# Second product last in the last pair, its last store on ScalarE's queue, two warm-up matmuls fewer, and all steps in another order

## The chip, the core and the metric

The kernel runs on one core of a Trainium2 chip. The core has a matrix engine (TensorE, in the profile PE, its weight loads PEld), a vector engine (VectorE, DVE), an activation engine (ScalarE, ACT), a general engine (GpSimd, POOL) and a queue engine that issues most transfers (SyncE, SP). Each takes its own instructions in program order and waits on semaphores for the others. The metric is the device time of one execution in microseconds. The kernel before took 226.16 us, the median of 3 runs (226.01 to 226.32).

## The reference

One transformer layer on 2048 tokens of width 640, in bf16: layer norm, linear attention with 32 heads of width 20 and a softmax feature map, a residual, a second layer norm, and a feed-forward part of width 1728 with SiLU.

```
h  = x + A(layernorm(x))          # A: q, k, v = x @ wqkv
                                  #    phi(u) = [softmax(u @ w_phi), softmax(-(u @ w_phi))]
                                  #    kv = sum_s phi(k) v ; z = sum_s phi(k)
                                  #    o = phi(q) kv / (phi(q) z + 1e-6) ; o @ wo
h2 = h + silu(layernorm(h) @ w1) @ w2
```

## The kernel before

The 2048 tokens are 16 tiles of 128. The program is built of some nine hundred small named steps, each a function that emits a few instructions. A list, `ORDER` (lines 18 to 61), written out by hand or by a search outside the kernel, gives the order in which the steps are emitted, and so the order of the instructions on each engine; nothing else reorders them. Several functions take PSUM banks from a ring in the order in which they are called (lines 124 to 147), so `ORDER` also decides which step waits for which bank.

The steps that the text names:

- `warm0` and on (line 229): matmuls on a constant, 128x256, whose result nobody reads. There are `WARM = 20` (line 150), 18 at the very beginning, one after `fk2` and one before `fk0`.
- `X0, X1, X2, X4, X8`, `WK0` to `WK4`, `WV0` to `WV4`, `wq0` to `wq5`, `wph0`, `wph1`, `load0` to `load10`: loads, all issued from SP. `wq` are loads that transpose (line 425). `X8` brings the tokens 8 to 15 of every partition, 1280 KB.
- `wk0` to `wk4` (line 323): five TensorE transposes each of a part of the key weights `Wk`; `wke0` to `wke4` copy them out of PSUM. `fk0` to `fk4` (line 339) multiply them by the block-diagonal feature weights `phi`, `fk0e` to `fk4e` copy the result into `Wfk`. `fq0` to `fq5` with `fq0e` to `fq5e` do the same for the queries, from `phq` and `wq`.
- `st{t}` (line 474): mean and variance of tile t on VectorE. `rs{t}`: their inverse root, on GpSimd or ScalarE. `xn{t}`: the normalised tile. `xt{t}`: its transpose, by TensorE for the first four (copied out by `x{t}`), by a DMA from SP for the others.
- `K{t}`, `V{t}` (line 566): key and value projections, ten matmuls each. `ex{t}` (ScalarE) exponentials, `su{t}` (VectorE) their sums, `rk{t}` (ScalarE) the reciprocals, `sc{t}` (VectorE, line 641) the scaling, `ve{t}` (ScalarE) the values out of PSUM, `kv{t}` (line 656) the eleven matmuls that add tile t into the key-value sums. `kv{t}` needs `sc{t}`.
- `own`, `mask`, `mask0`, `mask1`, `ones0` to `ones6`, `pad0`, `ref5` to `ref15`: constants and buffer resets on GpSimd. `ref{t}` writes again into the buffer of keys that tile t-5 used, so it waits for `kv{t-5}`. `eqr0`, `eqr1` (line 457) write the constant slots of `EQ`, the buffer of the queries' exponentials.
- `Q{t}` (line 705): query projections; `qe{t}` exponentials, `qs`, `ql`, `qi`, `qr` sums and scaling, `qt{t}` the transpose by DMA. `D{t}`, `E{t}`, `ot{t}`: attention, division, transpose. `G{t}0`, `G{t}1`, `ga{t}`: output projection and residual. `lm, ls, lr, hn, ht`: the second layer norm and its transpose.
- `u{a}.{f}`, `s{a}.{f}`, `lt{a}` (lines 924 to 981): the first feed-forward product, SiLU, and the transpose of its last rows.
- The second feed-forward product works on pairs of tiles with Strassen's scheme in Winograd's form, seven products instead of eight: `T` (sums of weights), `S1` to `S4` (sums of tokens, on VectorE), `p1` to `p7` (products, seven matmuls each, line 1024), `r1, r2, r3, r7` (a product plus the residual, out of PSUM, line 1041), `w11, w12, w21, w22` (the four quarters of the output, line 1048). Products accumulate: `p1`, then `p6`, then `p5` go into one bank "a", and `r1`, `r2`, `r3` read it after the first, second and third; `p7` and `p4` share bank "d"; `p2` and `p3` have banks of their own, and only `w11` reads `p2`, only `w12` reads `p3`.
- `out{t}` (line 983): the store of a tile's output, from SP. In the last pair (t = 14) the store of tile 14 is cut into `out140`, `out141`, `out142`, and product p3 with its quarter w12 into two parts, `p3.14` (192 columns) and `p3.14x` (128 columns), `w12.14` and `w12.14x`.

Of the kernel before, what the change touches and what calls it, by code (L numbers as in the profile page):

```python
# [18 lines left out]
warm0 warm1 warm2 warm3 warm4 warm5 warm6 warm7 warm8 warm9 warm10 warm11 warm12 warm13 warm14 pad0
warm15 warm16 X0 WK2 st0 WK3 warm17 WK0 phi_a X1 wk2 own wke2 phi_b wk3 fk2 rs0 xn0 warm18 ones0 WK1  # L20
mask wke3 WK4 X2 WV0 wk0 wk1 fk2e WV3 wke0 st1 xt0 wke1 rs1 wk4 fk3 X4 fk3e x0 fk1 wke4 xn1 ones1 warm19
st2 fk0 wq4 WV2 V0.0 fk1e WV1 fk4 ones4 xt1 fk0e K0s st3 mask0 V0.3 fk4e x1 WV4 ones3 K0.2 K0.1 K0.0
wph0 K0.4 rs3 rs2 st4 K0.3 K1 V0.2 xn2 xt2 st5 ex0 rs4 ex1 V0.1 wph1 x2 V1 X8 ve1 xn3 xt3 su0 st6 rk0
xn4 V0.4 su1 x3 load10 ones5 wq0 sc0 K2 st7 rs5 st9 ve0 V2 xn5 rs6 xt4 xn6 ex2 rk1 sc1 ve2 ones2 rs9
st12 wq3 xt5 phq V3 kv0 rs7 ve3 xt6 K3 K4 xn7 V4 ref5 kv1 ex3 ex4 st8 rs8 su2 su3 ve4 fq0 fq0e V5 fq3
ref6 st10 rk2 xn8 ve5 wq2 K5 xn9 rk3 xt7 fq3e sc2 ex5 K6 ex6 kv2 wq1 sc3 su4 kv3 ref7 V6 su5 fq2 rk4 ve6
K7 V7 rs12 fq2e ref8 su6 xn12 sc4 kv4 fq1 rs10 ex7 ve7 xt8 st15 rk6 ones6 xt9 fq1e zeros V8 st11 su7 fq4
xn10 st14 ref9 ve8 rs11 wq5 sc6 rk5 fq4e xt12 xt10 rk7 V9 load7 sc5 ve9 K8 xn11 K9 sc7 fq5 kv5 fq5e kv6
load3 kv7 ex8 ex9 st13 rs14 rs13 eqr0 su8 Q0 qe0 su9 ref10 rk8 rk9 xn13 K10 ref12 xn14 ex10 xt11 V10 sc8
ve10 ref11 load9 Q1 kv8 V12 rs15 xn15 xt13 K12 qs0 qe1 su10 sc9 kv9 rk10 ve12 ref13 K11 load1 ex12 K13  # L30
ex11 sc10 qs1 su12 xt14 ql0 ex13 ql1 V11 su11 su13 eqr1 rk12 rk11 load4 qi0 ve11 kv10 K14 xt15 sc11 rk13
V13 ref14 sc12 eqp qr0 qi1 ex14 ve13 qr1 sc13 ref15 K15 load0 Q2 ex15 load2 kv11 kv12 su14 kv13 su15 V15
qe2 qt0 rk14 qt1 rk15 V14 sc14 ve14 sc15 mask1 load8 ve15 Q3 qs2 kv14 ql2 kv15 Q5 bd0 qe3 qe5 Q7 bd1
load5 qi2 halves qr2 qe7 D0 D1 qs3 ql3 E0 load6 Q4 qe4 Q10 qi3 qt2 E1 qr3 qs5 qe10 qs4 ql5 Q6 qe6 ot0 D2
ot1 Q9 qe9 qi5 ql4 qr5 E2 G00 G01 ga0 lm0 ls0 qi4 G11 G10 qt3 Q11 qs6 qr4 D3 ga1 qe11 qt5 E3 lm1 lr0 hn0
Q8 ls1 D5 ot2 qt4 Q13 qr6 G20 qs7 lr1 G21 qe8 hn1 Q14 qe13 E5 Q15 qe14 ot3 Q12 ga2 G31 G30 ht0 qe15 qe12
padL0 qs8 ht1 D4 u0.L ot5 T1.2 T1.0 qr7 s0.L T1.1 u0.0 lm2 padL1 qt6 ga3 E4 qt7 u0.6 qs9 G50 s0.0 qr8
lm3 G51 T2.1 s0.6 D6 u0.4 ls2 s0.4 ga5 E6 u0.8 D7 ot4 lr2 lm5 qt8 u0.10 T3.2 u0.2 E7 G41 G40 ls5 hn2
u0.12 ot6 s0.2 T2.2 D8 lr5 s0.8 T3.1 T3.0 lt0 ls3 S3.0 s0.10 ga4 hn5 E8 s0.12 ot7 T2.0 p7.0 S1.0 G61
p1.0 T4.1 S2.0 p2.0 r1.0 r7.0 G60 ht2 p6.0 T4.0 T4.2 lr3 p4.0 G71 S4.0 r2.0 p3.0 lm4 p5.0 qr9 ls4 lr4  # L40
G70 ga6 hn3 ht5 w21.0 qs11 hn4 w22.0 ga7 ht3 ht4 u2.L lm6 u2.9 s2.L u2.1 qt9 r3.0 u2.7 ot8 w11.0 lm7
w12.0 lt2 qr11 u2.10 s2.9 qs10 G81 qt11 s2.1 qr10 qs12 D9 u2.3 s2.3 s2.7 qt10 G80 E9 u2.5 ls6 lr6 u2.4
s2.10 u2.2 ga8 u2.6 D10 ls7 u2.0 ot9 qr12 qt12 qs13 u2.12 s2.4 E10 lm8 D11 hn6 s2.5 ls8 ot10 u2.8 s2.0
qs14 E11 s2.6 s2.12 lr7 lr8 u2.11 G90 qr13 s2.2 D12 hn7 hn8 S3.2 ht6 s2.8 G91 p7.2 G101 qr14 ga9 s2.11
S1.2 p1.2 S2.2 E12 G100 r1.2 out0 p2.2 ga10 qt13 ot11 lm9 p6.2 qt14 S4.2 D13 r2.2 r7.2 G110 G111 w11.2
ls9 out1 S3.4 p4.2 E13 p5.2 ot12 ga11 lr9 w21.2 ht7 hn9 ht9 ht8 w22.2 ot13 D14 p7.4 r3.2 E14 lm11 p3.2
qs15 S1.4 p1.4 S2.4 ls11 G121 r1.4 lm10 u6.L ls10 G120 u6.8 lr10 p6.4 r7.4 p4.4 ga12 S4.4 r2.4 lm12 qr15
G131 w12.2 ot14 w21.4 G130 ga13 qt15 s6.L hn10 ls12 ht10 p5.4 lr11 s6.8 u6.11 G140 lm13 hn11 s6.11 u6.4
s6.4 lr12 D15 G141 u6.2 hn12 ls13 out3 r3.4 w22.4 p2.4 u6.5 s6.5 s6.2 E15 ga14 lr13 hn13 u6.1 w11.4 ht12
u6.0 u6.3 lt6 u6.10 u6.7 out2 s6.10 s6.7 s6.3 s6.1 p3.4 w12.4 ht11 ht13 u6.6 s6.0 u10.L ot15 u6.12 u10.2  # L50
s6.12 u10.9 s10.L G151 G150 s6.6 u6.9 S3.6 s10.2 u10.11 s6.9 S1.6 ga15 S2.6 lm15 u10.0 p7.6 s10.9 p1.6
u10.6 lt10 lm14 S3.8 r1.6 s10.0 r7.6 s10.11 u10.7 s10.6 s10.7 u10.12 p4.6 S4.6 p6.6 p2.6 s10.12 r2.6
p5.6 r3.6 ls15 w11.6 w21.6 u10.5 p2.8 S1.8 ls14 u10.3 w22.6 out5 lr15 u10.1 s10.5 p7.8 lr14 p1.8 S2.8
s10.3 hn14 u10.4 hn15 s10.1 r1.8 s10.4 ht14 w11.8 S3.10 p3.6 p6.8 ht15 r7.8 S4.8 u10.8 p4.8 out4 u14.4
r2.8 w21.8 w12.6 s14.4 u10.10 p5.8 s10.8 w22.8 p3.8 r3.8 out6 u14.2 out9 w12.8 s14.2 s10.10 S1.10 u14.12
p7.10 u14.10 out7 u14.L s14.12 u14.0 u14.6 p1.10 out8 S3.12 s14.0 s14.L r7.10 lt14 u14.8 S2.10 r1.10
s14.6 p6.10 p4.10 s14.10 r2.10 p5.10 w21.10 r3.10 S4.10 p2.10 p7.12 p2.12 w11.10 w22.10 S1.12 p1.12
S2.12 r1.12 w11.12 p3.10 p6.12 r7.12 p4.12 S4.12 r2.12 S3.14 w21.12 s14.8 w12.10 p5.12 p1.14 out11 r3.12
# [6 lines left out]
def kernel(  # L65
# [160 lines left out]
    def add(name, emit):  # L226
        steps[name] = emit
# [752 lines left out]
            sh_l.pop(u)[:, 0:m].rearrange("p j f -> p (j f)"),  # L980
        )

    def store(t, a, b):
        nc.sync.dma_start(out_t[:, t, a:b], outs[t][:, a:b])

# [38 lines left out]
    def product(t, k, lo=0, hi=HD):  # L1024
        bank = INTO[k] + "x" * (lo > 0)
        if k in FIRST:
            ps_of[bank, t] = ps_half()
# [6 lines left out]
        right = {1: b11, 2: b21, 3: b22, 4: ws.get(4), 5: ws.get(1), 6: ws.get(2), 7: ws.get(3)}[k]
        for c in range(KS):
            nc.tensor.matmul(  # L1036
                ps[:, lo:hi], left[:, c, :], right[:, c, lo:hi], start=(c == 0 and k in FIRST),
                stop=(c == KS - 1 and k in LAST), skip_group_check=True,
            )
# [95 lines left out]
```

## Time and profile before

| | us |
|---|---|
| median of 3 runs | 226.16 (226.01 to 226.32) |
| the profiled execution | 226.19 |
| its span in the trace | 224.5 |
| TensorE busy | 219.7 (98%) |
| VectorE busy | 173.9 (77%) |
| ScalarE busy | 144.8 (65%) |
| GpSimd busy | 72.5 (32%) |
| chain that ended last, TensorE's share | 87% |
| the same, VectorE's share | 11% |

The span runs from the first instruction to the last; some 1.7 us of the execution lie outside it. A row of the timeline gives a start in microseconds from the start of the span, a duration, the engine, the line of the kernel, the operation, out<-in with the shape of one, and how many instructions of a line follow each other directly; a bracket at its end is the idle time of the engine before it and what ended that. DVEq, SPq and so on are the sequencer of an engine: waits, branches, and the issue of transfers. Matmuls overlap and their ends are modelled, so the time that one takes is read from the start of one to the start of the next.

### The profile page before, as it was taken

How to read it: one execution, taken by the hardware profiler on the slowest of the kernel's cores; microseconds unless marked ns; L12 is line 12 of the kernel's file. 1: busy time of each engine (PE TensorE's matmuls, PEld its weight loads, DVE VectorE, ACT ScalarE, POOL GpSimd, SP SyncE). 2: the span in 40 equal slices, each digit the busy share in tenths (PEclk: the TensorE clock that was granted, in tenths of full speed). 3: DMA queues.
4: the chain of work that ended last, by engine and by line, in shares of the span. 5: the costliest groups of instructions: out<-in, count | busy, mean ns of one | idle time of the engine just before them, and what ended most of it. 6: DMA issues, size and time to landing. Idle time of an engine off the chain costs nothing.

```text
span 224.5 us, 5053 instructions
## 1 busy us (share of the span) xinstructions
PE 219.7 (98%) x1937; PEld 155.1 (69%) x1937; DVE 173.9 (77%) x305; ACT 144.8 (65%) x321; POOL 72.5 (32%) x136
## 2 busy tenths in 40 slices
...
GB/s 171 293 357 81 92 95 86 204 243 145 286 222 191 164 144 90 163 90 114 121 119 131 112 174 128 44 123 101 72 53 0 0 4 88 92 29 10 29 50 99
DMA packets 68158, 26.98 MB, mean 120 GB/s; under 512 B 61159, under 2 KB 67111, under 8 KB 68007
## 3 DMA queue, kind: packets, MB, share of 16 engines
...
q10 hardware_dynamic: 656, 0.03, 0.2%
q14 instruction: 8, 0.07, 0.1%
...
## 4 chain that ended last, share of the span: by engine, by line
PE 87%; DVE 11%; issue 0%; DVEq 0%
PE banks L931 25%; PE banks L1036 23%; PE banks L571 11%; PE banks L849 10%; PE banks L609 9%; DVE st L478 4%; PE banks L817 3%; DVE Sk L630 2%; PE banks L662 2%; PE banks L231 2%; DVE xn L494 1%; DVE EK L643 1%; PE banks L942 1%; DVE mv L479 1%; DVE WTk L338 0%; PE banks L437 0%
## 5 line engine op out<-in xcount | busy, mean ns | idle before, releaser
L931 PE MATMUL banks<-HnT,w_sb 128*128 128x512 bf16 (+1 forms) x325 | 60.7, 336 | 0.0
L954 ACT ACTIVATE shT<-banks 128x512 bf16<-128x512 f32 (+1 forms) x53 | 29.5, 587 | 32.1 <-PE banks L931 31.9
L931 PEld LDWEIGHTS <-w_sb 128*128 128x128 bf16 x325 | 31.2, 98 | 21.2
L571 PEld LDWEIGHTS <-XnT 128*128 128x128 bf16 x300 | 28.7, 98 | 9.6
L494 POOL TENSOR_SCALAR xn<-X,mv,rs 128x640 bf16<-128x640 bf16 x12 | 32.4, 2701 | 1.6 <-ACT rs L485 1.3
L516 POOL TENSOR_SCALAR rs<-mv 128x1 f32<-128x1 f32 x16 | 3.5, 219 | 80.2 <-ACT xn L509 79.9
L1036 PEld LDWEIGHTS <-S 128*128 128x128 bf16 x231 | 22.1, 98 | 9.0
L1044 DVE TENSOR_TENSOR r<-banks,X 128x320 f32<-128x320 f32 x32 | 15.2, 486 | 15.9 <-PE banks L1036 15.5
L1036 PE MATMUL banks<-T,S 128*128 128x320 bf16 x168 | 26.7, 299 | 0.0
L849 PE MATMUL banks<-wo_sb,OT 128*128 128x320 bf16 x160 | 25.3, 299 | 0.0
L1051 DVE TENSOR_TENSOR o_t<-banks,r 128x320 bf16<-128x320 f32 (+2 forms) x33 | 14.9, 475 | 12.6 <-PE banks L1036 12.2
L737 DVE TENSOR_REDUCE Sq<-EQ 128x66 f32<-128x1320 bf16 x16 | 24.2, 1519 | 0.0
L609 PE MATMUL banks<-Wfq,XnT 128*128 128x342 bf16 (+2 forms) x160 | 22.7, 293 | 0.0
L571 PE MATMUL banks<-Wv,XnT 128*128 128x320 bf16 x150 | 22.5, 299 | 0.0
L630 DVE TENSOR_REDUCE Sk<-EK 128x64 f32<-128x1216 bf16 x16 | 21.9, 1396 | 0.0
L733 ACT ACTIVATE EQ<-banks 128x342 bf16<-128x342 f32 (+2 forms) x52 | 21.4, 531 | 0.5 <-DMA w_sb<-in_B_w_dram 0.5
L1036 PEld LDWEIGHTS <-shT 128*128 128x128 bf16 x168 | 16.4, 98 | 7.0
L571 PE MATMUL banks<-Wfk,XnT 128*128 128x304 bf16 x150 | 21.2, 292 | 0.0
L626 ACT ACTIVATE EK<-banks 128x608 bf16<-128x608 f32 x32 | 20.1, 699 | 0.3 <-PE banks L571 0.3
L504 ACT ACTIVATE xn<-X 128x640 bf16<-128x640 bf16 x16 | 11.8, 737 | 12.8 <-DVE X L856 12.4
L849 PEld LDWEIGHTS <-OT 128*128 128x128 bf16 x160 | 15.3, 98 | 6.4
L609 PEld LDWEIGHTS <-XnT 128*128 128x128 bf16 x160 | 15.0, 97 | 5.5
...
## 6 DMA issues: line engine op xcount, KB each, us to landing
...
X<-in_A_x_dram SPq DMA_DIRECT2D x1, 1280.0 KB, 8.3
...
```

The costliest lines, as they stand in the source:

```text
L494: eng.tensor_scalar(out=xn_[t][:], in0=X[:, t, :], scalar1=mv_.pop(t)[:, 0:1], scalar2=rs_.pop(t)[:], op0=ALU.subtract, op1=ALU.mult,)
L571: nc.tensor.matmul(ps[:, g, 0:w], XnT[:, c, t * P : (t + 1) * P], W[:, c, g * w : (g + 1) * w], start=(c == 0), stop=(c == C - 1),)
L609: nc.tensor.matmul(ps[:, 0 : e - a], XnT[:, c, t * P : (t + 1) * P], Wfq[:, c, a:e], start=(c == 0), stop=(c == C - 1),)
L626: nc.scalar.activation(E5[:, :, :, b, 0:DR], p4, AF.Exp, scale=sign)
L630: nc.vector.tensor_reduce(sk[t][:], ek[t][:, 0 : H * HF].rearrange("p (q f) -> p q f", f=DH)[:, :, 0:DR], axis=AX.X, op=ALU.add)
L733: nc.scalar.activation(features(t, a, b)[:, :, :, i, 0:DR], p4, AF.Exp, scale=sign)
L737: nc.vector.tensor_reduce(sq[t][:], EQ[0][:, t, :, 0:FCH].rearrange("p c (q f) -> p c q f", f=DH), axis=AX.X, op=ALU.add)
L849: nc.tensor.matmul(ps_of["G", t][:, g, 0:HD], ot[t][:, c, :], wo_sb[:, c, g * HD : (g + 1) * HD], start=(c == 0), stop=(c == C - 1),)
L931: nc.tensor.matmul(ps[:, at : at + n], w1_sb[:, c, fc * P : fc * P + P], HnT[u][:, c, 0:n], start=(c == 0), stop=(c == C - 1),)
L954: nc.scalar.activation(rows_of(u)[:, f0 * n : f1 * n], ps_of.pop(("u", u, f0))[:, 0 : (f1 - f0) * n], AF.Silu)
L1036: nc.tensor.matmul(ps[:, lo:hi], left[:, c, :], right[:, c, lo:hi], start=(c == 0 and k in FIRST), stop=(c == KS - 1 and k in LAST), skip_ ...
L1044: nc.vector.tensor_tensor(r_[t, name][:], ps_of[bank, t][:, 0:HD], X[:, t + i, g * HD : (g + 1) * HD], op=ALU.add)
```

## The change

Four things change.

`WARM` is 18 instead of 20. Of the 18, 17 stand at the beginning and one, `warm17`, between `wk2` and `wk3`; those after `fk2` and before `fk0` are gone.

In the last pair, p2 and w11 are cut into two parts in place of p3 and w12, and p2 is the last product. TensorE's last steps before and after:

```
before  p1.14 p7.14 p3.12 p2.14 p6.14 p4.14 p5.14 p3.14x p3.14
after   p1.14 p4.12 p3.12 p7.14 p6.14 p4.14 p5.14 p3.14 p2.14 p2.14x
```

VectorE's last steps are `w21.14 w11.14 w22.14 r3.14 w12.14x w12.14` before and `w21.14 w22.14 r3.14 w12.14 w11.14 w11.14x` after.

The store of tile 14 is cut at other columns (320 to 640, 0 to 192, 192 to 320), and the last of the three, 128 columns, is issued from ScalarE's queue instead of SP's. It is ScalarE's last instruction.

All of `ORDER` is another order. At the head, by engine:

```
TensorE before  wk2 wk3 fk2 warm18 wk0 wk1 xt0 wk4 fk3 fk1 warm19 fk0 V0.0 fk4 xt1 V0.3 K0 K1 V0.2 xt2 V0.1 V1 xt3 V0.4
        after   wk2 warm17 wk3 fk2 wk0 xt0 wk1 fk3 wk4 fk0 fk1 V0.0 fk4 xt1 V0.3 K0 K1 V0.2 xt2 V0.1 V1 xt3 V0.4
        before  K2 V2 V3 kv0 K3 K4 V4 kv1 fq0 V5 fq3 K5 K6 kv2 kv3 V6 fq2 K7 V7 kv4 fq1 V8 fq4 V9 K8 K9 fq5 kv5 kv6 kv7 Q0 K10 V10 Q1
        after   K2 V2 K3 kv0 V3 K4 V4 fq0 V5 kv1 fq3 K5 K6 kv2 V6 fq2 K7 V7 kv3 fq1 V8 kv4 fq4 V9 K8 kv5 K9 fq5 kv6 Q0 kv7 K10 V10 Q1
VectorE before  wke2 phi_b xn0 st1 wke1 x0 wke4 xn1 st2 st3 st4 xn2 st5 su0 st6 su1 sc0 st7 st9 xn6 sc1 st12 st8 su2 su3 st10 sc2 sc3
        after   wke2 phi_b xn0 st1 wke1 x0 wke4 xn1 st2 st3 st4 xn2 st6 st5 su0 xn6 su1 sc0 st7 st9 st10 st8 sc1 su2 st14 su3 sc2 su4 st11 st12 sc3
ScalarE before  wke3 fk2e wke0 rs1 fk3e fk1e fk0e fk4e x1 rs3 ex0 rs4 ex1 x2 ve1 rk0 x3 ve0 rs6 ex2 rk1 ve2 rs9 rs7 ve3 ex3 ex4
        after   wke3 fk2e wke0 rs1 fk3e fk0e fk1e fk4e x1 rs3 ex0 rs4 ex1 x2 rs6 ve1 rk0 x3 ve0 ex2 ve2 ex3 rs7 rk1 ve3 ex4
GpSimd  before  pad0 own rs0 ones0 mask ones1 ones4 mask0 ones3 rs2 xn3 xn4 ones5 rs5 xn5 ... xn9 ref7 ref8 xn12 rs10 ones6 zeros xn10 ref9 xn11 eqr0
        after   ones5 mask ones4 rs0 ones0 ones3 pad0 ones1 mask0 own rs2 xn3 xn4 rs5 xn5 ... xn9 ref7 rs10 xn10 zeros ref8 ref9 xn12 ones6 ref10 xn11 eqr0
SP      before  X2 WV0 WV3 X4 wq4 WV2 WV1 WV4 wph0 wph1 X8 load10 wq0 xt4 wq3 xt5 xt6 wq2 xt7 wq1
        after   X2 WV0 WV3 X4 WV2 wph0 WV1 WV4 wph1 wq3 wq0 X8 xt4 wq1 xt5 xt6 wq2 xt7 wq4
```

In the first pair TensorE's order is `p7.0 G61 p1.0 p2.0 G60 p6.0 p4.0 G71 p3.0 p5.0` before and `p7.0 G61 G60 p1.0 p2.0 G71 G70 p6.0 p4.0 p5.0 p3.0` after; VectorE's after is `r7.0 S1.0 r1.0 S2.0 qr9 S4.0 r2.0`.

The diff, without the list:

```diff
-    WARM = 20
+    WARM = 18
...
-    def store(t, a, b):
-        nc.sync.dma_start(out_t[:, t, a:b], outs[t][:, a:b])
+    def store(t, a, b, queue=None):
+        (queue or nc.sync).dma_start(out_t[:, t, a:b], outs[t][:, a:b])
...
         for k in range(1, 8):
-            if k != 3:
+            if k != 2:
                 add(f"p{k}.{t}", lambda t=t, k=k: product(t, k))
         for j, (lo, hi) in enumerate(cuts):
-            add(f"p3.{t}" + "x" * j, lambda t=t, lo=lo, hi=hi: product(t, 3, lo, hi))
-            add(f"w12.{t}" + "x" * j, lambda t=t, lo=lo, hi=hi: added(t, "r3", "b" + "x" * (lo > 0), 0, 1, lo, hi))
+            add(f"p2.{t}" + "x" * j, lambda t=t, lo=lo, hi=hi: product(t, 2, lo, hi))
+            add(f"w11.{t}" + "x" * j, lambda t=t, lo=lo, hi=hi: added(t, "r1", "c" + "x" * (lo > 0), 0, 0, lo, hi))
...
-        add(f"w11.{t}", lambda t=t: added(t, "r1", "c", 0, 0))
+        add(f"w12.{t}", lambda t=t: added(t, "r3", "b", 0, 1))
...
-                for g, (lo, hi) in enumerate(((0, HD), (HD, HD + 192), (HD + 192, D))):
-                    add(f"out{t}{g}", lambda t=t, lo=lo, hi=hi: store(t, lo, hi))
+                for g, (lo, hi) in enumerate(((HD, D), (0, 192), (192, HD))):
+                    add(f"out{t}{g}", lambda t=t, lo=lo, hi=hi, q=nc.scalar if lo == 192 else None: store(t, lo, hi, q))
```

More of the change, by code (lines that the diff above doesn't have):

```diff
@@ L18 @@
 ORDER = """
[L19 to L58, printed above, removed]
@@ L59 @@
-p7.14 S1.14 p3.12 S2.14 p2.14 r1.14 p6.14 w22.12 r7.14 out10 S4.14 w12.12 p4.14 r2.14 p5.14 w21.14
-w11.14 out12 p3.14x w22.14 p3.14 r3.14 w12.14x out13 out140 out15 out142 w12.14 out141
+warm0 warm1 warm2 warm3 warm4 warm5 warm6 warm7 warm8 warm9 warm10 warm11 warm12 warm13 warm14 warm15
+warm16 X0 WK2 st0 wk2 ones5 WK3 phi_a warm17 WK0 wke2 X1 phi_b wk3 mask fk2 wke3 ones4 WK1 WK4 wk0 rs0
+xn0 xt0 fk2e wk1 X2 WV0 WV3 st1 X4 wke0 wke1 WV2 fk3 wph0 wk4 ones0 rs1 ones3 fk3e WV1 pad0 ones1 x0
+wke4 fk0 fk1 V0.0 fk0e fk4 xn1 xt1 V0.3 WV4 fk1e K0s K0.2 st2 st3 fk4e K0.1 wph1 x1 mask0 K0.0 st4 rs3
@@ new lines @@
+own K0.4 rs2 xn2 K0.3 ex0 K1 V0.2 rs4 xn3 st6 xt2 ex1 V0.1 wq3 V1 wq0 xt3 x2 rs6 V0.4 ve1 X8 st5 xn4 su0
+xn6 su1 rk0 sc0 x3 xt4 st7 K2 ve0 V2 ex2 st9 rs5 wq1 xn5 st10 ve2 K3 xt5 kv0 ex3 rs7 V3 rk1 ve3 st8
+ones2 sc1 phq xn7 su2 K4 ex4 st14 V4 fq0 V5 rs8 ve4 fq0e xt6 kv1 su3 rk2 ve5 rs9 fq3 ref6 fq3e sc2 wq2
+ref5 K5 xt7 su4 K6 ex5 kv2 st11 V6 xn8 xn9 ex6 st12 rk3 ref7 fq2 sc3 wq4 su5 K7 ve6 rk4 xt8 xt9 fq2e ex7
+sc4 V7 rs10 su6 xn10 kv3 rs11 rs12 fq1 V8 ve7 kv4 su7 fq1e zeros ref8 fq4 ve8 V9 rk5 K8 fq4e rk6 ref9
```

33 lines of the change are left out of this document (added).

## The prediction

> **What bounds the kernel now.** I read the page's head first, then the windows, then the chain of waits in order of time, then the timeline around each place that the change touches.
>
> ```profile
> span 224.5 us, 5053 instructions
> ```
>
> ```profile
> 4.60:9.00 4.40, 3.96 (x48) 3.03 (x46) 4.14 (x9) 2.40 (x6) 3.61 (x17) 1.00 0.93 317
> 9.00:30.00 21.00, 20.80 (x208) 16.09 (x206) 20.66 (x44) 20.55 (x49) 17.61 (x20) 1.00 0.86 181
> 120.00:205.00 85.00, 85.00 (x643) 54.34 (x641) 46.29 (x87) 43.99 (x88) 10.21 (x28) 1.00 0.35 74
> ```
>
> The windows give each stretch, its length, then PE, PEld, DVE, ACT, POOL busy and the granted clock. TensorE has almost no idle time, so the same matmuls in another order gain only where it waits now, and lose wherever the new order makes it wait. It waits in the first 9 us (3.96 busy of 4.40) and a little before 30 us. From 9 to 30 us VectorE and ScalarE are as full as TensorE (20.66 and 20.55 of 21.00), so TensorE cannot run far ahead of them. After 120 us both are half empty.
>
> ```profile
> 0.82 4.00 PE banks L231 x18
> 4.83 0.55 PE banks L321 x5
> ...
> 28.52 1.44 DVE EK L643 x2
> ```
>
> In this chain the warm-ups set when the first transposes (step wk2) run; these set VectorE's copy (wke2), and nearly all of what follows to 29.96 us is VectorE's. There TensorE takes over.
>
> **The front.** Two warm-ups go and one more is put behind wk2, so 17 instead of 18 stand ahead of it. wk2's last transpose releases wke2.
>
> ```profile
> 4.62 1.32 PE L321 MATMUL banks<-ident,Wk 128*128 128x128 bf16 x10
> ```
>
> ```profile
> 5.40 0.49 DVE L338 COPY WTk<-banks 128x640 bf16<-128x640 bf16 x1 [0.23 <-PE banks L321]
> ```
>
> ```profile
> DMA to landing us min/median/max: 2.6/3.6/4.0
> ```
>
> The 18 warm-ups start at 0.82 and wk2 at 4.62: 3.80 / 18 = 0.21 us each. wk2 needs Wk's first part, issued at 1.2. By the landing row (of the tile Wk) it lands between 3.8 (1.2 + 2.6) and 5.2 (1.2 + 4.0). I take 3.8, since the first of five loads has the fewest ahead of it; then wk2 starts at 4.41, and VectorE, which now idles 0.23 us for it, starts everything behind it 0.21 us earlier. Had that load been the slowest, the gain is 0. The warm-up behind wk2 falls into the pause before wk3, which waits for its own weights; uncovered it would cost 0.21. The two that go between folds lie beside waits for VectorE: 0.
>
> TensorE's own gain up to its third transpose of xn (xt2) is the smaller of what it saves and what VectorE allows:
>
> ```profile
> 12.87 0.81 DVE L494 TENSOR_SCALAR xn<-X,mv,rs 128x640 bf16<-128x640 bf16 x1
> ```
>
> ```profile
> 13.77 0.44 PE L530 MATMUL banks<-ident,xn 128*128 128x128 bf16 x5
> ```
>
> VectorE's steps up to xn2 stand in the same order, so xn2 ends at 13.68 - 0.21 = 13.47, and xt2 starts at 13.53 instead of 13.77: **-0.24 us** (bounds 0 and -0.30). GpSimd's mask steps ("own") move behind the first normalisation's scale and end near the start of xn1; if they overlap it, xn1 may grow as xn2 (0.81) has beside GpSimd's work, and take this term. The loads of Wv move up on SP past the transposing load wq4; TensorE waits for none of them now.
>
> **The stall at 30 us.**
>
> ```profile
> 29.30 0.50 PE L662 MATMUL banks<-VP,EK 128*128 128x63 bf16 x11
> 30.00 0.51 PE L662 MATMUL banks<-VP,EK 128*128 128x63 bf16 x11 [0.20 <-DVE EK L643]
> 30.35 1.52 PE L571 MATMUL banks<-Wv,XnT 128*128 128x320 bf16 x10
> 31.71 0.41 PE L437 MATMUL banks<-phi_q,WTq 128*128 128x114 bf16 x5
> ...
> 33.25 1.52 PE L571 MATMUL banks<-Wv,XnT 128*128 128x320 bf16 x10
> 34.73 0.51 PE L662 MATMUL banks<-VP,EK 128*128 128x63 bf16 x11
> ```
>
> kv3 follows kv2 directly and waits for sc3. A kv takes 30.35 - 30.00 = 0.35 of TensorE, so kv2 is over at 29.65 and 0.35 us are lost; V7 takes what V6 takes (30.35 to 31.71: 1.36), is over at 34.61, and kv4 loses 0.12. In the new order V6, fq2, K7 and V7 stand before kv3: 34.61 - 30.35 = 4.26 us later. sc3 moves back too, behind su4, st11 and st12.
>
> ```profile
> 16.96 1.37 DVE L630 TENSOR_REDUCE Sk<-EK 128x64 f32<-128x1216 bf16 x1
> 18.24 0.81 DVE L643 TENSOR_TENSOR EK<-EK,Rk 128x1280 bf16<-128x1280 bf16 x1
> ```
>
> ```profile
> 20.01 0.83 DVE L478 BATCH_NORM_STATS2 st<-X 128x6 f32<-128x320 bf16 x2
> ```
>
> ```profile
> 21.00 0.96 DVE L494 TENSOR_SCALAR xn<-X,mv,rs 128x640 bf16<-128x640 bf16 x1
> 21.88 0.95 DVE L643 TENSOR_TENSOR EK<-EK,Rk 128x1280 bf16<-128x1280 bf16 x1
> ```
>
> A su takes 1.28 (16.96 to 18.24), an st 0.99 (20.01 to 21.00): 1.28 + 2 x 0.99 = 3.26, covered by 4.26. kv4 stands behind one more projection as well. So **-0.47 us** (bounds -0.47 and 0).
>
> **What is given back.** TensorE, 0.71 us earlier, meets the first query's exponentials (qe0), which the change does not bring forward.
>
> ```profile
> 43.35 0.56 POOL L460 MEMSET EQ<- 128x264 f32 x1
> ```
>
> ```profile
> 43.95 1.32 ACT L733 ACTIVATE EQ<-banks 128x627 bf16<-128x627 f32 x2 [0.51 <-DMA w_sb<-in_B_w_dram]
> ```
>
> ```profile
> 45.98 1.47 PE L609 MATMUL banks<-Wfq,XnT 128*128 128x342 bf16 x10
> ```
>
> The trace names a DMA for qe0's wait, but qe0 starts as GpSimd's memset of EQ ends (43.35 + 0.56 = 43.91). In the new order GpSimd has one reset (ref10) more and ones5 less before it, and ref9, which waits for kv4, stands ahead of xn12; I estimate qe0 at 44.1. Q1 (the third row) takes Q0's banks, free at 44.1 + 1.32 = 45.4, and would otherwise start at 45.98 - 0.71 = 45.27. With its semaphores about **+0.20 us** (bounds 0, if GpSimd follows TensorE's shift, and +0.71, if all is lost there).
>
> **From 60 to 205 us** steps change places nearly everywhere, but the last window shows no idle time to gain. Tight spots are new: in the first pair p5.0 now follows p6.0 and p4.0 directly and needs bank a read by r2.0, which VectorE does only after qr9 and S4.0. I put **+0.10 us** for such places (bounds 0 and +0.6, not quite two stalls like kv3's).
>
> **The end.** The last pair's products end p5, p3, p2 (192 columns), p2 (128) instead of p5, p3 (128), p3 (192).
>
> ```profile
> 220.01 1.13 PE L1036 MATMUL banks<-w_sb,S 128*128 128x128 bf16 x14
> ```
>
> ```profile
> 221.20 0.56 DVE L1051 TENSOR_TENSOR o_t<-banks,r 128x128 bf16<-128x128 f32 x2
> 221.52 0.81 SPq L984 DMA_DIRECT2D out_dram<-o_t  x2
> ```
>
> ```profile
> L1051 DVE TENSOR_TENSOR o_t<-banks,r x2: 292/320/347, 221.2 to 221.4; 128x128 bf16<-128x128 f32 x1, 128x192 bf16<-128x192 f32 x1
> ```
>
> ```profile
> out_dram<-o_t SPq DMA_DIRECT2D x1, 32.0 KB, 1.5
> ```
>
> ```profile
> DMA to landing us min/median/max: 2.7/2.7/2.7
> ```
>
> TensorE ends at 221.14. r3 ahead of them holds the two adds, 0.29 and 0.35 long, until 221.20, and the second ends at 221.76. SP sends the two stores from 221.52 to 222.33, so the last starts near 221.9. In the new order w22 and r3 run beside p3, w12 beside p2, and only the 128-column add follows TensorE's end: 221.20 + 0.29 = 221.49. ScalarE is idle by then and nothing is queued behind the store there; it can issue at 221.52, as SP did after the same add: 0.4 us earlier. A store of this size takes 1.5 us from SP; ScalarE's only DMA of the trace, the load of WPH, took 2.7 (last row). Had the store ScalarE's 2.7, the end would be 0.8 later. Of the bounds -0.4 and +0.8 I take **-0.35**, by the same store's row, with a little for the other queue. The 192-column store leaves SP near 221.2 and lands before.
>
> The Trainium skill ("DMA: Bandwidth & Descriptors", "Issuing engines are not separate DMA queues") says that DMAs of all issuers end on the same 16 DMA engines, and that a second issuer saves only issue time. By it the term would be -0.4; the WPH row, a load among others, says less.
>
> **Sum:** -0.24 - 0.47 + 0.20 + 0.10 - 0.35 = -0.76. The profiled execution took 226.19 (224.5 of span and 1.7 around it), 0.03 over the median of the runs: 226.16 - 0.76 = **225.4 us**. With 0.1 for the front, 0.2 for what is given back and 0.1 for the end either way, its own range is 225.0 to 225.8.
>
> **Rivals.**
> A. All of the front is lost again before 60 us: the end remains, 226.16 - 0.35 = 225.8. For it: three engines are full there, and the give-back's bound is 0.71. Against: kv3's stall is plainly removed.
>
> B. Slower: X arrives late. X's last 1280 KB now stand on SP behind two transposing loads of WTq (wq3, wq0) instead of one (wq4).
>
> ```profile
> X<-in_A_x_dram SPq DMA_DIRECT2D x1, 1280.0 KB, 8.3
> ```
>
> ```profile
> 5.97 1.41 SPq L425 DMA_TRANSPOSE WTq<-in_A_wqkv_dram  x1
> ```
>
> ```profile
> 10.30 0.58 SPq L178 DMA_DIRECT2D X<-in_A_x_dram  x1
> ```
>
> One load of 1.41 more puts their issue at 11.7 and, with the 8.3 of now, their landing at 20.0; st9 asks for them at 20.01 - 0.21 + 0.88 (xn6, 21.00 to 21.88, now before it) = 20.7. From there each us of lateness goes through VectorE to TensorE: landed at 22.2 it costs 1.5, and the time is 226.9; it decides from 21.9. Against: the 8.3 us are mostly other loads ahead.
>
> C. Slower: the clock is released later.
>
> ```profile
> 6.58 0.72 PE L321 MATMUL banks<-ident,Wk 128*128 128x128 bf16 x10
> ```
>
> Ten transposes take 1.32 us from 4.62 and 0.72 from 6.58: the pace doubles in between. The first window has 3.96 us busy; less the 0.78 up to the pause before wk3 and the overlap of matmuls, whose ends are modelled, I estimate 1.9 us of matmuls up to 9 us, which at half pace would take 1.9 more, 0.7 of it in waits that are there now: 225.4 + 1.2 = 226.6. It decides from a release 0.9 late. Against: with the moved warm-up, 18 still stand ahead of wk3. The Trainium skill ("TensorE: Matmul & The Clock Gate", "What's actually happening" and "Part 4: PE-mode transpose") has a free-running window of activity and does not count transposes as busy, which speaks for it.
>
> D. ScalarE's store gains nothing: 226.16 - 0.41 = 225.8.
>
> **Chances.** Forecast 0.62, A 0.13, D 0.07, B 0.06, C 0.05, and 0.07 for stalls after 60 us beyond their bound (226.3 and more). Under 0.2% (0.45 us) no measurement of this kernel tells from no change: faster is below 225.7, slower above 226.6. Faster: nine tenths of the forecast and three of A and D, 0.62. Slower: B, half of C and of the stalls, 0.12. Same: 0.26. The range leaves out B, C and the far stalls: 224.8 to 226.3.
>
> **What would show it.** Right: wke2 at 5.2; kv2 and kv3 apart and no idle TensorE around 30 us; Q1 starting as qe0 ends; the last store on ScalarE's queue 0.4 after TensorE's end, landing within 1.6. Wrong: wk2 waits for its load, xn1 takes 0.8, TensorE stalls between 60 and 205 us, or the last store takes 2 us and more.

## The result, and the profile after

The changed kernel took **225.38 us** (median of 5 runs, 224.91 to 225.49) against 226.16 (226.01 to 226.32, 5 runs). The ratio is put at 0.9959, with a 95% interval of 0.9944 to 0.9975; that of the two medians is 0.9966. The profiled execution took 225.49, with a span of 223.8 (before: 226.19 and 224.5). First the page's head and the engines' shares of its chain of waits:

```profile
span 223.8 us, 5031 instructions
...
PE 94%; DMA 2%; SPq 2%; issue 0%; DVE 0%
```

VectorE's 11% of the chain are gone; what stands beside TensorE now is a load and the queue that issues it. The window from 9 to 30 us says where (length, then PE, PEld, DVE, ACT, POOL busy, granted clock):

```profile
9.00:30.00 21.00, 20.06 (x194) 15.36 (x194) 19.75 (x40) 19.14 (x45) 17.54 (x21) 1.00 0.75 182
```

There TensorE is busy 20.06 instead of 20.80, and VectorE and ScalarE have 0.9 and 1.4 us less as well. The timeline of the front, TensorE (with its third transpose of xn, xt2, last), then VectorE and the last of GpSimd's resets beside xn0:

```profile
7.95 0.85 PE L345 MATMUL banks<-phi,WTk 128*128 128x228 bf16 x8
9.94 0.43 PE L583 MATMUL banks<-Wv,XnT 128*128 128x320 bf16 x2 [1.15 <-DMA Wv<-in_A_wqkv_dram]
...
13.99 0.39 PE L530 MATMUL banks<-ident,xn 128*128 128x128 bf16 x4
...
5.08 0.48 DVE L338 COPY WTk<-banks 128x640 bf16<-128x640 bf16 x1
5.86 0.56 DVE L494 TENSOR_SCALAR xn<-X,mv,rs 128x640 bf16<-128x640 bf16 x1
...
8.51 0.43 DVE L494 TENSOR_SCALAR xn<-X,mv,rs 128x640 bf16<-128x640 bf16 x1
9.51 0.89 DVE L478 BATCH_NORM_STATS2 st<-X 128x6 f32<-128x320 bf16 x2 [0.56 <-DMA X<-in_A_x_dram]
...
12.03 0.89 DVE L478 BATCH_NORM_STATS2 st<-X 128x6 f32<-128x320 bf16 x2 [0.40 <-DMA X<-in_A_x_dram]
...
5.94 0.29 POOL L247 MEMSET EK<- 128x64 f32 x1
```

xn0, xn1 and that last reset in the kernel before:

```profile
6.19 1.20 DVE L494 TENSOR_SCALAR xn<-X,mv,rs 128x640 bf16<-128x640 bf16 x1
...
9.49 0.44 DVE L494 TENSOR_SCALAR xn<-X,mv,rs 128x640 bf16<-128x640 bf16 x1
...
6.91 0.30 POOL L247 MEMSET EK<- 128x64 f32 x1
```

wke2 starts at 5.08 (before: 5.40). xn0 takes 0.56 instead of 1.20, and xn1 starts at 8.51 (before: 9.49). In both kernels xn0 ends just behind the resets that GpSimd makes beside it: they end at 6.23 and xn0 at 6.42, before at 7.21 and 7.39. Then everything stops for loads: TensorE stands 1.15 us before V0.0 for the first fifth of Wv, VectorE 0.56 before st2 and 0.40 before st4 for X. xt2 starts at 13.99, 0.22 later than before.

Around 30 us:

```profile
29.66 0.51 PE L662 MATMUL banks<-VP,EK 128*128 128x63 bf16 x11
30.01 1.52 PE L571 MATMUL banks<-Wv,XnT 128*128 128x320 bf16 x10
31.36 0.41 PE L437 MATMUL banks<-phi_q,WTq 128*128 128x114 bf16 x5
31.61 1.46 PE L571 MATMUL banks<-Wfk,XnT 128*128 128x304 bf16 x10
32.91 1.52 PE L571 MATMUL banks<-Wv,XnT 128*128 128x320 bf16 x10
34.27 0.50 PE L662 MATMUL banks<-VP,EK 128*128 128x63 bf16 x11
...
36.80 0.43 PE L571 MATMUL banks<-Wv,XnT 128*128 128x320 bf16 x2
```

kv2 (29.66), V6, fq2, K7, V7 and kv3 (34.27) follow each other without a pause; the only wait left is 0.13 us before kv2. V9 (last row) starts at 36.80; in the kernel before, with the same steps behind it, it started at 36.94:

```profile
36.94 1.52 PE L571 MATMUL banks<-Wv,XnT 128*128 128x320 bf16 x10
```

GpSimd's xn11 and its reset of EQ, and ScalarE's qe0 with what stands around it:

```profile
40.14 2.50 POOL L494 TENSOR_SCALAR xn<-X,mv,rs 128x640 bf16<-128x640 bf16 x1
42.58 0.57 POOL L460 MEMSET EQ<- 128x264 f32 x1
...
43.72 0.31 ACT L639 ACTIVATE Rk<-Sk 128x128 bf16<-128x128 f32 x1
44.09 1.32 ACT L733 ACTIVATE EQ<-banks 128x627 bf16<-128x627 f32 x2
...
45.84 1.47 PE L609 MATMUL banks<-Wfq,XnT 128*128 128x342 bf16 x10
```

The reset is over at 43.15 instead of 43.91, and qe0 no longer waits for it: ScalarE does the reciprocals of tile 8 first (rk8, two instructions; the second is the row above qe0). Q1 starts at 45.84, 0.43 after qe0's end. In the kernel before, xn11 ahead of the reset took 4.24 us instead of 2.50; why is not settled:

```profile
39.17 4.24 POOL L494 TENSOR_SCALAR xn<-X,mv,rs 128x640 bf16<-128x640 bf16 x1
```

The end:

```profile
219.76 1.13 PE L1036 MATMUL banks<-w_sb,shT 128*128 128x192 bf16 x14
219.99 1.23 DVE L1051 TENSOR_TENSOR o_t<-banks,r 128x320 bf16<-128x320 f32 x3
220.50 0.81 SPq L984 DMA_DIRECT2D out_dram<-o_t  x2
221.25 0.36 ACTq L984 DMA_DIRECT2D out_dram<-o_t  x1
```

TensorE ends at 220.89, the last add at 220.93 + 0.29 = 221.22, ScalarE issues at 221.25, and that store lands at 222.78 by the trace's records, 1.53 after its issue.

So, with the same work behind each point, the changed kernel stands against the kernel before (profiled executions):

| place | before | after | difference | of which new | predicted |
|---|---|---|---|---|---|
| xt2 | 13.77 | 13.99 | +0.22 | front +0.22 | -0.24 |
| V9 | 36.94 | 36.80 | -0.14 | stall -0.36 | -0.47 |
| Q1 | 45.98 | 45.84 | -0.14 | given back 0 | +0.20 |
| TensorE's end | 221.14 | 220.89 | -0.25 | 46 us to the end -0.11 | +0.10 |
| span | 224.5 | 223.8 | -0.70 | the end -0.45 | -0.35 |

### The profile page after: what moved, and what is told of

The parts are those of the page before. It is cut to its first block, busy times and chain, and to the rows that moved or that the text cites. A ratio compares the mean times of both kernels' runs of the same rounds, so it can differ in the third digit from the quotient of the medians.

```text
span 223.8 us, 5031 instructions
## 1 busy us (share of the span) xinstructions
PE 218.2 (98%) x1926; PEld 154.8 (69%) x1935; DVE 173.0 (77%) x305; ACT 144.4 (65%) x321; POOL 70.2 (31%) x136
## 4 chain that ended last, share of the span: by engine, by line
PE 94%; DMA 2%; SPq 2%; issue 0%; DVE 0%
PE banks L931 25%; PE banks L1036 24%; PE banks L571 18%; PE banks L849 10%; PE banks L609 9%; PE banks L817 3%; PE banks L662 2%; DMA Wv<-in_A_wqkv_dram 2%; PE banks L942 1%; SPq L181 1%; PE banks L583 1%; PE banks L437 1%; PE banks L598 1%; SPq L178 1%; PE banks L530 0%
## 5 line engine op out<-in xcount | busy, mean ns | idle before, releaser
L931 PE MATMUL banks<-HnT,w_sb 128*128 128x512 bf16 (+1 forms) x316 | 60.0, 335 | 0.4
L494 POOL TENSOR_SCALAR xn<-X,mv,rs 128x640 bf16<-128x640 bf16 x12 | 30.6, 2550 | 1.7 <-ACT rs L485 1.4
L1036 PEld LDWEIGHTS <-S 128*128 128x128 bf16 x224 | 21.6, 98 | 8.8
L1036 PE MATMUL banks<-T,S 128*128 128x320 bf16 x168 | 26.1, 299 | 0.0
L1018 DVE TENSOR_TENSOR S<-shT 128x896 bf16<-128x896 bf16 x16 | 9.8, 619 | 12.5 <-ACT shT L954 8.8
```

What stands on the lines that cost most here:

```text
L494: eng.tensor_scalar(out=xn_[t][:], in0=X[:, t, :], scalar1=mv_.pop(t)[:, 0:1], scalar2=rs_.pop(t)[:], op0=ALU.subtract, op1=ALU.mult,)
L931: nc.tensor.matmul(ps[:, at : at + n], w1_sb[:, c, fc * P : fc * P + P], HnT[u][:, c, 0:n], start=(c == 0), stop=(c == C - 1),)
L1036: nc.tensor.matmul(ps[:, lo:hi], left[:, c, :], right[:, c, lo:hi], start=(c == 0 and k in FIRST), stop=(c == KS - 1 and k in LAST), skip_ ...
```

## The experiments

Twelve runs, each timed beside runs of the kernel before on the same chip (medians of those: 226.19 to 226.21). "After" and "before" in the diffs are the two kernels of this document.

| run | us, median (lowest to highest, runs) | ratio to before, 95% |
|---|---|---|
| the changed kernel again | 225.32 (224.82 to 225.81, 6) | 0.9949 to 0.9974 |
| new end alone | 225.79 (225.53 to 225.84, 11) | 0.9974 to 0.9991 |
| all but the new end | 225.87 (225.73 to 226.42, 11) | 0.9986 to 1.0003 |
| old order of loads | 225.13 (224.84 to 225.42, 5) | 0.9938 to 0.9964 |
| last store on SP | 225.67 (224.96 to 226.54, 12) | 0.9959 to 0.9990 |
| kv3 behind V6 | 226.20 (225.59 to 226.32, 12) | 0.9989 to 1.0014 |
| V0.0 behind xt1 | 225.00 (224.70 to 225.81, 12) | 0.9937 to 0.9966 |
| and st4 behind xn2 | 224.78 (224.48 to 225.21, 6) | 0.9919 to 0.9961 |
| warm-ups alone | 226.20 (225.60 to 226.31, 11) | 0.9987 to 1.0006 |
| kv3 and kv4 moved | 226.21 (226.05 to 227.42, 11) | 0.9997 to 1.0020 |
| new end, all on SP | 225.93 (225.29 to 227.32, 12) | 0.9979 to 1.0005 |
| V0.0 and st4 again | 224.72 (224.47 to 225.37, 5) | 0.9927 to 0.9956 |

### The front: order of the loads, or chance?

**The changed kernel again**, no edit.

> The changed kernel once more, unaltered. Theory (the new order of loads on SP makes X's third load and the first fifth of Wv land later): X2 lands near 9.5 us and V0.0 starts near 9.9 us again, 1.3 us of TensorE waiting; time 225.4. Rival (the landings of the head differ from one execution to the next by chance): X2 lands anywhere between 8.5 and 9.5 us, and with it at 8.6 the time is near 225.0.

```profile
9.66 0.43 PE L583 MATMUL banks<-Wv,XnT 128*128 128x320 bf16 x2 [0.60 <-DMA Wv<-in_A_wqkv_dram]
```

The wait is there again, half as long; X's third load lands at 9.22 instead of 9.49. The result repeats: with the first five, eleven runs have a median of 225.38 and lie between 224.82 and 225.81.

**Old order of loads.** In the changed kernel, the loads that SP issues behind X4, in their places in `ORDER`:

```diff
-WV2 wph0 WV1 WV4 wph1 wq3 wq0 X8 wq1 wq2 wq4
+wq4 WV2 WV1 WV4 wph0 wph1 X8 wq0 wq3 wq2 wq1
```

> The changed kernel with the loads on SP in the order of the kernel before (the transposing load wq4 right behind X4, then WV2, WV1, WV4, wph0, wph1, X8, and the other transposing loads), in the same places of the order. Theory (WV2, wph0 and WV1, issued 1.4 us earlier, share the DMA engines with X2 and WV0): X2 lands near 8.6 and WV0 near 9.0 us, V0.0 starts no later than 9.2, VectorE's st2 at 9.0, and the time falls by 0.3 to 0.45 to 225.0. Rival (chance): X2 lands as in the run of the changed kernel beside it, and the time is the same within 0.1.

WV0 lands at 9.17 and V0.0 starts at 9.21, as the theory has it, but the time, 225.13, lies within the changed kernel's own spread. For WV0 the profiles of two other kernels settle it. **kv3 behind V6** (below) has the loads of the kernel before, wq4 behind X4 on SP. Its answer for the first load of Wv alone:

```profile
L181 SPq DMA_DIRECT2D Wv<-in_A_wqkv_dram x1: 432/432/432, 4.5 to 4.5; - x1
...
DMA to landing us min/median/max: 5.4/5.4/5.4
```

That is as late as in the profile after. And **all but the new end** has the new loads:

```profile
9.06 0.43 PE L583 MATMUL banks<-Wv,XnT 128*128 128x320 bf16 x2
```

Here the same load landed 4.5 us after its issue, and V0.0 waited for nothing that the profile shows. The first eleven loads stand in the same order in every kernel of this study and up to WV0 leave SP at the same times (WV0 itself at 4.53 to 4.55); WV0 landed between 8.92 and 9.90, X2 between 8.54 and 9.49. With the old order of loads behind it WV0 landed at 8.96 to 9.90 (seven profiles, median 9.22), with the new one at 8.92 to 9.90 (seven, median 9.06), so that order is not the cause of a late WV0. The rival holds for it: the landings differ from one execution to the next, and the changed kernel, being ready for them earlier, now feels it.

X's fourth load, X4, is another matter. It landed at 11.28 to 12.01 with the old order behind it (median 11.60) and at 11.70 to 12.30 with the new one (median 11.99; trace's records, seven profiles each), and st4 waits for it 0.36 to 1.16 us in every profile with the new order. So the new order of loads seems to bring X4 some 0.4 us later. Whether that is the 0.25 by which 225.13 lies under 225.38, five runs do not tell.

**Warm-ups alone**, in the kernel before:

```diff
-    WARM = 20
+    WARM = 18
-warm15 warm16 X0 WK2 st0 WK3 warm17 WK0 phi_a X1 wk2 own wke2
+warm15 warm16 X0 WK2 st0 WK3 WK0 phi_a X1 wk2 warm17 own wke2
...
-fk2 rs0 xn0 warm18
+fk2 rs0 xn0
...
-ones1 warm19
+ones1
```

> The kernel before with the warm-ups alone changed: 18 instead of 20, 17 ahead of wk2 and one behind it. Theory (the head is bound by the loads of X and Wv, whose landing differs between executions): wke2 starts 0.2 earlier, st2, st4 and V0.0 begin when their loads land, xt2 at 13.6 to 14.0, and the time is 226.1 to 226.25. Rival (the prediction's term: VectorE carries the 0.21 to xt2): xt2 at 13.53, time 225.95.

The median does not move, as the theory said, but not for its reason: in the profile of the kernel before, once st0 has begun, no step up to xt2 waits for X or Wv. What holds VectorE there is xn0. Its row in kv3 behind V6 (below), which has the old head, and then in this run:

```profile
5.97 1.45 DVE L494 TENSOR_SCALAR xn<-X,mv,rs 128x640 bf16<-128x640 bf16 x1
```

```profile
5.91 0.81 DVE L494 TENSOR_SCALAR xn<-X,mv,rs 128x640 bf16<-128x640 bf16 x1
```

In kv3 behind V6 wke2 started at 5.11, 0.29 earlier than in the profile of the kernel before, and xn0 ended at 7.42 all the same (before: 7.39). In all five profiles with the kernel before's head and warm-ups xn0 ended at 7.39 to 7.44, 0.17 to 0.18 after the resets that GpSimd makes beside it. So an earlier wk2 alone gains nothing there. In this run's profile, the fastest of its eleven executions (225.60), xn0 ended at 6.71, ahead of the last resets, and all behind it came earlier: xt2 by 0.31 (13.46), GpSimd's reset of EQ by 0.58 (43.33), Q1 by 0.58 (45.40). An earlier end of xn0 is thus worth its time up to the end, but two warm-ups fewer do not bring it in most executions. The kernel before has fast executions too (225.53 at the lowest); whether xn0 is short in those no profile shows, and no run moved GpSimd's resets alone.

### The stall at 30 us

**kv3 behind V6**, in the kernel before:

```diff
-kv2 wq1 sc3 su4 kv3 ref7 V6 su5
+kv2 wq1 sc3 su4 V6 kv3 ref7 su5
```

> The kernel before with one swap alone: kv3 (and ref7) stand behind V6 instead of before it. Theory (the stall before kv3 is TensorE's own 0.35 us and is kept to the end): no wait before V6 or kv3, Q1 0.35 earlier, 226.19 - 0.35 = 225.85. Rival (given back at qe0 or Q1, as the prediction's term has it in part): Q1 starts less than 0.15 earlier, and the time is 226.05 to 226.2.

```profile
29.53 0.50 PE L662 MATMUL banks<-VP,EK 128*128 128x63 bf16 x11
29.87 1.52 PE L571 MATMUL banks<-Wv,XnT 128*128 128x320 bf16 x10
31.23 0.50 PE L662 MATMUL banks<-VP,EK 128*128 128x63 bf16 x11
...
33.11 1.52 PE L571 MATMUL banks<-Wv,XnT 128*128 128x320 bf16 x10
34.74 0.51 PE L662 MATMUL banks<-VP,EK 128*128 128x63 bf16 x11
...
33.86 0.82 DVE L643 TENSOR_TENSOR EK<-EK,Rk 128x1280 bf16<-128x1280 bf16 x1
```

kv3's wait is gone, and kv4 (34.74) waits 0.27 instead of 0.12: sc4 (last row) ends at 34.68, at the same time as in the kernel before. The time is unchanged. The rival was right about the time, by way of kv4 and not of Q1 (45.99).

**kv3 and kv4 moved**, in the kernel before:

```diff
-kv2 wq1 sc3 su4 kv3 ref7 V6
+kv2 wq1 sc3 su4 ref7 V6
...
-K7 V7 rs12 fq2e ref8 su6 xn12 sc4 kv4 fq1
+K7 V7 kv3 rs12 fq2e su6 xn12 ref8 sc4 fq1
...
-V8 st11
+V8 kv4 st11
```

> The kernel before with kv3 behind V7 and kv4 behind V8, as in the changed kernel (ref8 behind xn12). Theory (VectorE's sc4 at 34.7 us is what TensorE met at kv4 when kv3 alone was moved; with both behind a projection more there is 0.5 us of slack): no wait from V6 to V9, Q1 and D0 0.4 to 0.5 earlier, time 226.2 - 0.45 = 225.75. Rival (VectorE's pace holds TensorE at kv5 or Q1 instead): V9 earlier, Q1 not; time 226.1 to 226.2.

```profile
45.77 1.47 PE L609 MATMUL banks<-Wfq,XnT 128*128 128x342 bf16 x10
47.08 0.50 PE L662 MATMUL banks<-VP,EK 128*128 128x63 bf16 x11
47.65 0.57 PE L571 MATMUL banks<-Wv,XnT 128*128 128x320 bf16 x3
...
43.36 0.57 POOL L460 MEMSET EQ<- 128x264 f32 x1
...
43.96 1.32 ACT L733 ACTIVATE EQ<-banks 128x627 bf16<-128x627 f32 x2 [0.89 <-DMA w_sb<-in_B_w_dram]
...
46.33 1.26 ACT L626 ACTIVATE EK<-banks 128x608 bf16<-128x608 f32 x2
```

V9 and Q1 are 0.21 earlier (36.73, 45.77), and V12 (47.65) stands where it stood (47.63). It takes the banks that ex10 (last row) empties at 47.59; ex10 is behind qe0 on ScalarE, and qe0 waits for GpSimd's reset of EQ, which ends at 43.93 as it did in the kernel before (43.91). ScalarE's pause before qe0 has grown from 0.51 to 0.89: that is TensorE's gain, given back. The theory falls: in the kernel before the two waits of the kv steps cost nothing that could be had alone. The changed kernel keeps 0.36 of them up to V9 and on to Q1; by its profile that is because the reset is over 0.76 earlier there and rk8 stands ahead of qe0. No run moved the reset or rk8 alone.

### The end

**New end alone**, in the kernel before: the diff's parts behind `WARM` (the cut of p2 and w11, the three stores, ScalarE's queue), and

```diff
-S2.14 p2.14 r1.14 p6.14
+S2.14 r1.14 p6.14
...
-p5.14 w21.14 w11.14 out12 p3.14x w22.14 p3.14 r3.14 w12.14x out13 out140 out15 out142 w12.14 out141
+p5.14 out12 p3.14 p2.14 p2.14x w21.14 w22.14 out13 r3.14 out15 w12.14 w11.14 w11.14x out140 out141 out142
```

> The kernel before with nothing but the new end: product 2 last in the last pair, the three stores as in the changed kernel, the last from ScalarE's queue. Theory: from TensorE's end to the end of the span 2.9 us instead of 3.36, so 226.16 - 0.45 = 225.7 (225.6 to 225.8). Rival (most of the end's gain was TensorE's new order over the last pairs): the end of TensorE moves too, and the time falls by another 0.2 or none at all, 226.1.

TensorE ends at 221.17 (before: 221.14), and the span 2.9 later: the end alone is worth 226.19 - 225.79 = 0.40 us.

**New end, all on SP**: the same kernel, with

```diff
-add(f"out{t}{g}", lambda t=t, lo=lo, hi=hi, q=nc.scalar if lo == 192 else None: store(t, lo, hi, q))
+add(f"out{t}{g}", lambda t=t, lo=lo, hi=hi: store(t, lo, hi))
```

> The kernel before with the new end, its last store from SP as well. Theory (the store lands 0.16 later behind the other store's issue, and the closing after the last landing takes 0.97 us as in the kernel before): 225.79 + 0.16 = 225.95. Rival (with SP the closing takes 1.18 us, as in the run of the changed kernel with its last store on SP): 226.15, the whole gain of the end.

```profile
219.83 2.26 SPq L984 DMA_DIRECT2D out_dram<-o_t  x4
...
DMA to landing us min/median/max: 1.5/1.6/1.6
```

225.93: by the medians the second queue is worth 0.14, the order of the last products and adds 0.26. The store is issued at 221.71 instead of 221.53 and takes 1.54 us, as from ScalarE (1.52). Twelve runs have one of 227.32 among them, so the interval is wide and does not tell the two apart; the medians and the trace agree.

**Last store on SP**, in the changed kernel, by the same edit.

> The changed kernel with its very last store on SP's queue instead of ScalarE's; all else as changed. Theory (the end gains from the order of the products, the queue only saves the wait behind the 192-column store's issue): the store is issued 0.1 us later and lands 0.1 later, 225.3 + 0.1 = 225.4. Rival (the second queue carries the end's gain): the time rises by 0.35 to 0.45, to 225.7.

The median rises by 0.29 to 0.35, near the rival's number (the two ranges overlap widely). By the profile it is not for the rival's reason. The store lands 2.05 us after TensorE's end instead of 1.89 (trace's records), 0.16 later as in the run before; the rest is behind the last landing: from there to the end of the span it takes 1.19 us instead of 0.97 to 0.98. What happens in that closing isn't settled (see the last section).

**All but the new end**: the changed kernel with the old cut of p3 and w12, the old stores, and

```diff
-S2.14 r1.14
+S2.14 p2.14 r1.14
...
-p5.14 out10 p3.14 p2.14 p2.14x w21.14 w22.14 out13 out12 r3.14 out15 w12.14 w11.14 w11.14x out140 out141 out142
+p5.14 out10 w21.14 w11.14 p3.14x w22.14 p3.14 out13 out12 r3.14 w12.14x out140 out15 out142 w12.14 out141
```

> The changed kernel with the old end: product 3 last in the last pair, all three last stores from SP. Theory: the end costs 0.45 again, 225.38 + 0.45 = 225.8 (225.7 to 225.95), 0.3 under the kernel before, which is the gain of the front and of the stall at 30 us. Rival (the end is worth 0.8 and nothing else gains): 226.15, as before.

225.87 is what the theory gave, but the split is not clean: six of the eleven runs lie under 225.9, four at 226.29 and above, and in the profile VectorE works through from 217.8 to 220.4 us without a pause (the kernel before has two, 0.64 and 0.46, up to 219.3) and finishes 0.84 us after TensorE instead of 0.62. The closing takes 1.18 here as well. The interval of this run includes no change, so it does not show by itself that anything is left without the end. The new end alone does: its eleven runs (225.53 to 225.84, median 225.79) leave 0.41 to the changed kernel's median of 225.38.

### A faster version

If loads bound the front, TensorE and VectorE should do first what needs none. **V0.0 behind xt1**, in the changed kernel, and, in a second kernel, **st4 behind xn2** as well:

```diff
-wke4 fk0 fk1 V0.0 fk0e fk4 xn1 xt1 V0.3
+wke4 fk0 fk1 fk0e fk4 xn1 xt1 V0.0 V0.3
```

```diff
-K0.0 st4 rs3 own K0.4 rs2 xn2 K0.3
+K0.0 rs3 own K0.4 rs2 xn2 st4 K0.3
```

> The changed kernel with V0.0 moved behind fk4 and xt1 on TensorE, so that these two (0.65 us) run while Wv's first fifth is still on its way. Theory (the load of Wv is what TensorE waits for at 9 us): the wait at V0.0 shrinks to 0.7 or nothing, fk4e starts near 9.7 instead of 10.8 on ScalarE, xt2 0.3 to 0.5 earlier when the load lands late and equal when it lands early; 225.0, less spread. Rival (VectorE, through st4 and xn2, sets xt2 anyway): xt2 within 0.1 of the changed kernel's, 225.3.

> As the run with V0.0 behind xt1, and besides st4 moved behind xn2 on VectorE, so that xn2 no longer waits for X's fourth load (12.0 us). Theory (two loads, WV0 and X4, bound the front): xn2 starts near 11.7, xt2 follows TensorE alone near 13.3, 224.9 or less. Rival (VectorE is full from 13 to 28 us, and st4 only waits in another place): xt3 and K2 stand where they stood, 225.3.

> The changed kernel with V0.0 behind xt1 and st4 behind xn2 once more, beside these runs. Theory: 224.8 again, 0.5 under the changed kernel. Rival (the six runs were a lucky draw of landings): 225.1 or more.

From the last run:

```profile
8.72 0.76 PE L345 MATMUL banks<-phi,WTk 128*128 128x133 bf16 x7
9.51 0.44 PE L530 MATMUL banks<-ident,xn 128*128 128x128 bf16 x5
9.78 0.71 PE L583 MATMUL banks<-Wv,XnT 128*128 128x320 bf16 x4
...
13.18 0.44 PE L530 MATMUL banks<-ident,xn 128*128 128x128 bf16 x5
...
11.11 0.45 DVE L494 TENSOR_SCALAR xn<-X,mv,rs 128x640 bf16<-128x640 bf16 x1
11.92 0.89 DVE L478 BATCH_NORM_STATS2 st<-X 128x6 f32<-128x320 bf16 x2 [0.36 <-DMA X<-in_A_x_dram]
```

fk4 and xt1 run ahead of V0.0, which finds its weights there; xn2 starts at 11.11 instead of 13.08, and only then st4 waits for X. xt2 starts at 13.18. In the first kernel it starts at 13.66: there st4 still stands ahead of xn2 and waits 1.06 us for X4. The first kernel takes 225.00; the second, over both its runs, 224.73 (median of eleven, 224.47 to 225.37), 0.65 under the changed kernel's eleven and 1.4 under the kernel before. (The changed kernel was not timed beside these two; the kernel before, timed beside each, had medians of 226.16 to 226.21.) How the gain divides between a load that is late and one that is not isn't shown: in the three profiles WV0 landed at 8.92, 9.26 and 8.98, early each time.

## Why the prediction was right, and where not

The time came out as forecast (225.4 for 225.38), but by luck to that degree: the front came out 0.46 worse than its term, and what was kept back in three others (0.20, 0.21 and 0.10), less 0.11 at the stall, made up for it.

**The front (-0.24, was +0.22)** failed. VectorE's chain moved up, wke2 to 5.08 (said 5.2) and xn1 by 1.0, but most of that is not wk2's doing: xn0 took 0.56 us instead of 1.20. It ends just behind GpSimd's resets in both, and these end 1.0 earlier; that they hold it is read from the profiles, not tried. The prediction moved xn0 as it stood; with the old order of these resets its end does not follow wke2 (7.39 and 7.42 for 5.40 and 5.11). The step that lost the term is "TensorE waits for none of them now": that was read from one execution in which WV0 landed at 8.96 and V0.0 started at 9.71. The same load may land at 9.90, and TensorE was due at 8.79. Where it landed at 9.90 in both orders, xt2 starts at 14.00 (kv3 behind V6) and 13.99 (the changed kernel): no gain, no loss. So +0.22 is the price of this execution and not of the order; all but the new end, with WV0 at 9.02, has xt2 at 13.22. The lower bound of the term, 0, stopped short of a loss, because the loads' price was taken from one execution. wk2 and its load were no issue: Wk's first part landed at 3.84, as taken. The growth of xn1 that was feared did not come here (0.43); with the old order of loads it did (0.84, beside GpSimd's part of "own").

**The stall (-0.47, was -0.36)** was sized rightly and explained too simply. Its two waits, 0.35 and 0.12, are gone and one of 0.13 before kv2 is new. But a wait taken away alone goes to kv4, and with kv4 moved it goes to V12; by the profiles the term needed the new order on GpSimd and ScalarE too.

**What is given back (+0.20, was 0)** named the true brake of the kernel before: GpSimd's reset of EQ, then qe0. The step that failed is that qe0 is something "which the change does not bring forward". The reset in front of it comes 0.76 earlier, above all because xn11 takes 2.50 us there instead of 4.24 (so in all eight profiles of the new order; 4.16 to 4.25 in the six of the old). And GpSimd now waits for TensorE: its resets ref9 and ref10 idle 0.53 and 0.42 us for kv steps. So the reset follows TensorE, which the prediction had as its bound of 0. In the eight profiles qe0 starts at 43.30 to 44.09, and Q1 always 1.75 or 1.76 later. That qe0 came at 44.09, for 44.1 said, is luck: TensorE was 0.57 later at V9 than the sum of the terms had it, and rk8 now stands ahead of qe0. Q1 did not start as qe0 ended, as the prediction's signs had it, but 0.43 later.

In the kernel before, the reset keeps its distance to the front and not to TensorE's kv steps: it ended 31.27 or 31.28 us after GpSimd's xn3 had started, in all six profiles. In kv3 behind V6 TensorE's xt2 was 0.23 late, xn3 was not (12.66; before 12.64), and Q1 was on time (45.99 to 45.98). In warm-ups alone xn3 was 0.58 early, and so was Q1.

**60 to 205 us (+0.10, was -0.11 from 46 us on)**: no stall came; two small waits of the kernel before (0.05 at kv9, 0.08 at Q2) went, both ahead of 60 us.

**The end (-0.35, was -0.45 in the profile and -0.40 alone)** was right, with too much kept back for the other queue. The Trainium skill's rule ("DMA: Bandwidth & Descriptors", "Issuing engines are not separate DMA queues") gave -0.4, and the trace agrees: from either queue the store takes 1.5 us, and what the second one saves, 0.14 to 0.16, is the other store's issue.

**The rivals.** A (all of the front lost) holds for the front, but the stall's gain stayed. B: X's last load was issued at 12.73, later than the 11.7 feared, and landed at 18.67 (trace's records), 5.9 us for the same load, so at least 2.4 of the 8.3 were not its own. C: the pace of the transposes doubled earlier, not later; wk3 ran at full pace from 5.25. Where it doubles differs between executions with the same warm-ups: with the 18 of the kernel before, wk2's transposes start 0.107 us apart in one profile and 0.056 in another (kv3 behind V6; trace's records), and with the changed kernel's, wk3's are still 0.10 apart in the run with the old order of loads, from 5.50. What the late release costs is not shown: that kernel's median is no higher than the changed kernel's, but its profile is the slowest of its five executions (225.42). Whether transposes count towards the release these runs don't tell. D is out by the last store.
